# Moving the transposes of chunks 8 to 23 from TensorE to DMA, in a retention layer followed by a squared-ReLU feed-forward block

## The chip, the cores and the metric

The kernel runs on one core of a Trainium2 chip. The metric is the device time of one execution in microseconds (us). "Span" is the time from the first to the last instruction in the profile; a run takes about 1.8 us more than its span. Before: 227.94 us, median of 3 runs (227.5 to 228.03). PE is TensorE, PEld its weight loads, DVE is VectorE, ACT ScalarE, POOL GpSimd, and SPq is the instruction queue of SyncE, which issues most of the DMA transfers. "Half clock" below means that the profile shows a granted TensorE clock of 0.5.

## The reference

```python
# q, k, v: (4, 8, 768, 64), i.e. batch, heads, sequence, head dimension
gamma = 1.0 - 2.0 ** (-5.0 - np.arange(H))
for t in range(S):
    state = gamma * state + outer(k[t], v[t])          # per batch and head
    y[:, :, t] = (1/sqrt(64)) * q[t] @ state
x = y.transpose(0, 2, 1, 3).reshape(3072, 512)
h = np.maximum(x @ w_in, 0)                             # 512 -> 2048
out = (h * h) @ w_out                                   # 2048 -> 512
```

The kernel does the recurrence in 24 chunks of 128 time steps (6 per batch element). In a chunk, the scores of k against q are one matrix product, masked to the causal triangle; the state carries what came before. The decay is split into a factor on k and one on the query side. The feed-forward block is the bulk of the matmuls.

## The kernel before

For each chunk `m` a program string calls small steps: `K` casts, `T` transposes k and q, `S` makes the scores and masks them, `P` makes the output and the new state, `F` is a hidden tile (16 per block of chunks), `G` a quarter of an output tile, `Z` filler matmuls that keep TensorE busy at the start, `L` loads. The order is by hand: each engine executes its instructions in exactly this order.

```python
blocks = (2, 2, 1, 3, 4, 4, 4, 4)          # chunks per feed-forward block

def a_cast(m):                              # "K"
    nc.vector.scalar_tensor_tensor(out=ks[:], in0=kn.pop(m)[:], scalar=scale,
        in1=kf[:, i, :, None].to_broadcast([P, H, D]), op0=ALU.mult, op1=ALU.mult)
    if m < FIRST:                           # FIRST = 8
        # q: ScalarE for m < 4, GpSimd for 4 to 7; v: GpSimd
    ...                                     # from chunk 8 on the loads of q and v cast

def a_turn(m):                              # "T"
    for x, src in enumerate((a["ks"], a["qs"])):
        for p in range(NP):
            nc.tensor.transpose(tp[:, x, p, :], src[:, 2 * p : 2 * p + 2, :], ident[:])
    nc.scalar.activation(kqT[:], tp[:], AF.Copy)

def a_out(m, after=None):                   # "P"
    ...                                     # state, value and update matmuls
    nc.vector.tensor_tensor(out=xts[g][:, :, j * P : (j + 1) * P],
                            in0=yt[:], in1=yf[i][:], op=ALU.mult)   # yf: decay table
    ...
# yf[i] is filled by four Exp on ScalarE ("Y"), six tables in all
run("F0.0 P3 Y5 F0.1 F0.2 F0.3 F1.0 F1.1 F1.2 F1.3")
```

## Time and profile before

| | before |
|---|---|
| run, median | 227.94 us |
| span of the profile | 225.9 us |
| PE busy | 212.3 us, 94% |
| DVE, ACT busy | 46%, 54% |
| first hidden matmul | 19.46 us |
| first output matmul | 35.61 us |
| first hidden matmul of chunks 8 to 11 | 94.64 us |
| first hidden matmul of the last block | 194.48 us |
| end of the matmuls | 222.28 us |

The last rows are stage marks, read from the timeline of PE.

The page, part 1 (busy us, share of the span, instructions) and part 2 (busy tenths in 40 equal slices), kernel before:

```profile
PE 212.3 (94%) x1736; PEld 117.5 (52%) x1736; DVE 103.2 (46%) x221; ACT 123.1 (54%) x246; POOL 43.5 (19%) x62
...
PE   7677899998879999999999999999999999999993
```

From about the thirteenth slice on (some 68 us; a slice is 5.65 us) PE is full: there each microsecond of PE work taken away should come off the end. Before it, PE waits. The waits of PE, kernel before; the columns are the waiting instruction, what ended the wait, total us, times, longest:

```profile
PE tp_1119 L217 <- DVE ks_1116 L192: 1.3, 1, 1.3
PE hp_0_499 L316 <- ACT h_0_442 L323: 1.2, 1, 1.2
...
PE st_923 L227 <- ACT kqT_891 L218: 0.4, 1, 0.4
PE st_1055 L227 <- ACT kqT_1023 L218: 0.4, 1, 0.4
PE st_783 L227 <- ACT kqT_767 L218: 0.3, 1, 0.3
PE yt_862 L264 <- DVE pt_847 L235: 0.3, 1, 0.3
...
PE yt_981 L264 <- DVE pt_932 L235: 0.2, 1, 0.2
```

The 1.2 us of `hp_0_499` lies at 22.2 us, where ScalarE fills the last decay table:

The timeline of ACT, kernel before (start us, us, engine, line, operation):

```profile
20.87 0.77 ACT L297 ACTIVATE s_bd_174<-c_260 64x256 bf16<-64x256 f32 x2 [0.37 <-PE c_260 L280]
21.65 1.28 ACT L172 ACTIVATE yf_173<-t_f,lnp 128x128 f32<-128x128 f32 x4
22.95 0.38 ACT L323 ACTIVATE h_0_442<-hp_1_478 128x256 bf16<-128x256 f32 x1
```

The eviction of the second hidden tile starts only at 22.95 us, though that tile was made by 21.3 us; PE runs out of PSUM buffers (three for hidden and output tiles). What a chunk's transposes cost is seen where PE is full (timeline of PE, kernel before):

```profile
161.46 0.39 PE L217 MATMUL tp_2338<-ident,ks_2265 128*128 128x128 bf16 x4
161.69 0.39 PE L217 MATMUL tp_2338<-ident,qs_2079 128*128 128x128 bf16 x4
161.91 1.03 PE L316 MATMUL hp_0_2349<-xt_1995,w_in_bf_96 128*128 128x512 bf16 x4
```

From start to start the eight transposes hold PE for 161.91 - 161.46 = 0.45 us (0.445 over several chunks; the durations overlap, so they are not to be summed).

### The profile page before, as it was taken

The page shows a single profiled execution, that of the slowest core. Times are in us where ns is not written, and L with a number is a line of the kernel's source. Part 1 is how long each engine was busy: PE and PEld are TensorE (multiplying, and loading weights), DVE is VectorE, ACT ScalarE, POOL GpSimd, SP SyncE. Part 2 cuts the span into 40 slices and gives each one's busy share as a digit, 9 for nine tenths or more (in the row PEclk, how much of TensorE's full clock was granted, in tenths as well). Part 3 has the DMA queues.
Part 4 walks back from the last instruction along what each step waited for, and adds up shares of the span by engine and source line. Part 5 has one row for each costly group of instructions (what it writes and reads, how often), then busy time and mean ns, then how long its engine had stood idle before and what let it go on. Part 6 is the DMA issues. An engine that isn't in the chain of part 4 may idle for free.

```text
span 225.9 us, 4271 instructions
## 1 busy us (share of the span) xinstructions
PE 212.3 (94%) x1736; PEld 117.5 (52%) x1736; DVE 103.2 (46%) x221; ACT 123.1 (54%) x246; POOL 43.5 (19%) x62
## 2 busy tenths in 40 slices
PE   7677899998879999999999999999999999999993
PEld 2444785456646664445455555455454555444441
DVE  4574664127835964175650275740275704144000
ACT  6798883156637862377623477524467532367121
POOL 3275000439752433030330310000000000000000
PEclk9999999999999999999999999999999999999999
DMA  7999999989999999477729973013200011200112
GB/s 168 256 209 204 205 200 202 248 219 189 166 177 205 171 80 147 73 183 45 49 57 130 118 167 22 3 46 93 94 2 0 3 46 46 96 0 0 46 46 93
DMA packets 82579, 25.43 MB, mean 113 GB/s; under 512 B 75392, under 2 KB 79488, under 8 KB 82560
## 3 DMA queue, kind: packets, MB, share of 16 engines
q0 software_dynamic: 37504, 8.39, 40.7%
q1 hardware_dynamic: 45056, 16.78, 28.6%
q8 instruction: 13, 0.21, 0.4%
q14 instruction: 6, 0.05, 0.1%
HBM read 27.26 MB, written 6.29 MB: 149 GB/s over the span
## 4 chain that ended last, share of the span: by engine, by line
PE 84%; DMA 5%; ACT 4%; SPq 3%; DVE 2%; issue 1%; POOL 0%; ACTq 0%
DMA w_in_bf_96<-in_moe_w_in_dram 3%; SPq L91 3%; DMA vn_120<-in_v_dram 2%; PE op_2633 L335 2%; PE op_1480 L335 2%; PE op_2223 L335 2%; PE op_2512 L335 2%; PE op_2317 L335 2%; PE op_1920 L335 2%; PE op_1826 L335 2%; PE op_1427 L335 2%; PE op_1072 L335 2%; PE op_2860 L335 2%; PE op_705 L335 2%; PE op_695 L335 2%; PE op_2820 L335 2%
## 5 line engine op out<-in xcount | busy, mean ns | idle before, releaser
L316 PEld LDWEIGHTS <-w_in_bf_96 128*128 128x128 bf16 x128 | 11.4, 98 | 10.3 <-issue 1.4
L316 PEld LDWEIGHTS <-w_in_bf_98 128*128 128x128 bf16 x128 | 11.8, 98 | 8.7
L316 PEld LDWEIGHTS <-w_in_bf_99 128*128 128x128 bf16 x128 | 11.6, 98 | 8.2
L316 PEld LDWEIGHTS <-w_in_bf_97 128*128 128x128 bf16 x128 | 11.4, 98 | 8.1
L324 DVE TENSOR_TENSOR h_0_442<-h_0_442 128x256 bf16<-128x256 bf16 x32 | 9.3, 293 | 7.1 <-ACT h_0_442 L323 3.2
L324 DVE TENSOR_TENSOR h_5_2687<-h_5_2687 128x512 bf16<-128x512 bf16 x16 | 6.8, 426 | 11.8 <-ACT h_5_2687 L323 11.8
L324 DVE TENSOR_TENSOR h_2_1544<-h_2_1544 128x512 bf16<-128x512 bf16 x16 | 6.8, 424 | 10.7 <-ACT h_2_1544 L323 10.6
L324 DVE TENSOR_TENSOR h_4_2348<-h_4_2348 128x512 bf16<-128x512 bf16 x16 | 6.8, 425 | 9.6 <-ACT h_4_2348 L323 9.6
L324 DVE TENSOR_TENSOR h_3_1951<-h_3_1951 128x512 bf16<-128x512 bf16 x16 | 6.8, 423 | 9.5 <-ACT h_3_1951 L323 9.5
L324 DVE TENSOR_TENSOR h_1_876<-h_1_876 128x128 bf16<-128x128 bf16 (+1 forms) x32 | 8.2, 287 | 4.5 <-ACT h_1_876 L323 4.4
L335 PEld LDWEIGHTS <-h_5_2687 128*128 128x128 bf16 x64 | 6.3, 98 | 7.6
L335 PEld LDWEIGHTS <-h_3_1951 128*128 128x128 bf16 x64 | 6.0, 98 | 7.1
L335 PEld LDWEIGHTS <-h_2_1544 128*128 128x128 bf16 x64 | 6.0, 98 | 7.1
L335 PEld LDWEIGHTS <-h_4_2348 128*128 128x128 bf16 x64 | 5.9, 97 | 6.9
L335 PEld LDWEIGHTS <-h_1_876 128*128 128x128 bf16 x64 | 6.0, 98 | 6.8
L335 PEld LDWEIGHTS <-h_0_442 128*128 128x128 bf16 x64 | 6.0, 98 | 6.6
L351 PE MATMUL fill<-zero 128*128 128x512 bf16 x24 | 8.3, 484 | 1.2 <-DVE zero L146 1.2
L344 ACT ACTIVATE osb_744<-op_695 128x512 f32<-128x512 f32 x1 | 0.6, 597 | 8.2 <-PE op_695 L335 8.2
L253 PEld LDWEIGHTS <-s_bd_175 128*128 128x128 bf16 x48 | 3.6, 98 | 2.3
L351 PEld LDWEIGHTS <-zero 128*128 128x128 bf16 x24 | 2.4, 119 | 4.6 <-issue 2.7
L206 POOL CAST qs_736<-qn_420 128x512 bf16<-128x512 f32 x1 | 0.6, 613 | 19.6 <-DMA qn_420<-in_q_dram 19.6
L235 DVE TENSOR_TENSOR pt_792<-st_783,cmask 128x1024 bf16<-128x1024 f32 x1 | 1.2, 1225 | 5.8 <-PE st_783 L227 5.8
(811 smaller groups left out, 522.2 us busy)
## 6 DMA issues: line engine op xcount, KB each, us to landing
w_in_bf_96<-in_moe_w_in_dram POOLq DMA_DIRECT2D x1, 512.0 KB, 7.0
w_in_bf_97<-in_moe_w_in_dram POOLq DMA_DIRECT2D x1, 512.0 KB, 8.6
w_in_bf_98<-in_moe_w_in_dram POOLq DMA_DIRECT2D x1, 512.0 KB, 9.0
w_in_bf_99<-in_moe_w_in_dram POOLq DMA_DIRECT2D x1, 512.0 KB, 10.8
w_out_bf_100<-in_moe_w_out_dram POOLq DMA_DIRECT2D x1, 512.0 KB, 12.9
w_out_bf_101<-in_moe_w_out_dram POOLq DMA_DIRECT2D x1, 512.0 KB, 14.7
w_out_bf_102<-in_moe_w_out_dram POOLq DMA_DIRECT2D x1, 512.0 KB, 16.6
w_out_bf_103<-in_moe_w_out_dram POOLq DMA_DIRECT2D x1, 512.0 KB, 18.5
```

Of the source, the lines that this page charges most:

```text
L91: return eng.dma_start(t[:], src[b, :, i * C : (i + 1) * C, :].rearrange("h s d -> s h d"))
L206: nc.gpsimd.tensor_copy(qs[m][:], qn.pop(m)[:])
L235: nc.vector.tensor_tensor(out=pt[:], in0=st[:], in1=cmask[:, None, None, :].to_broadcast([P, 2, NP, P]), op=ALU.mult,)
L253: nc.tensor.matmul(yt[:, p, :], lhsT=s_bd[i % 2][:, p, :], rhs=kqT[:, 1, p, :], start=(p == 0), stop=False, skip_group_check=True,)
L316: nc.tensor.matmul(hp[:, :n], lhsT=w_in_bf[s][:, cb, r * P : (r + 1) * P], rhs=xts[g][:, cb, cols], start=(cb == 0), stop=(cb == NCB - 1),)
L324: nc.vector.tensor_mul(h2[:, fb, cols], h2[:, fb, cols], h2[:, fb, cols])
L335: nc.tensor.matmul(op[:], lhsT=h2s[g][:, fb, j * P : (j + 1) * P], rhs=w_out_bf[part][:, r, :], start=(fb == 0), stop=(fb == NFB - 1),)
L344: nc.scalar.activation(osb[:], op[:], AF.Copy)
L351: nc.tensor.matmul(t[:], lhsT=zero[:, :P], rhs=zero[:], start=True, stop=True)
```

## The change

Its intent: from chunk 8 on, k and q of a chunk, cast side by side into one tile, are transposed by one DMA transfer of 256 KB, issued by SyncE; TensorE and ScalarE are rid of it. The decay of the query side goes into the cast of q, on VectorE, so the decay tables and the multiplication of the output go; the output is copied by ScalarE. q is loaded as fp32 by SyncE (v still by the casting GpSimd queue), which gives SyncE four transfers a chunk: k, q, transpose, store. Blocks are 2-2-2-2-4-4-4-4. A 384-byte pad in front of the tiles aligns them. The PSUM buffer that was the transposes' own joins those of the hidden and output tiles, which become four. The schedule strings are rewritten. Cut to the core:

```diff
-    for n in (2, 2, 1, 3, 4, 4, 4, 4):
+    for n in (2, 2, 2, 2, 4, 4, 4, 4):
...
+    pad = wpool.tile([P, 192], BF16)
+    nc.vector.memset(pad[:], 0.0)
...
-    ps_f = ctx.enter_context(tc.tile_pool(name="ps_f", bufs=3, space=PS))
+    ps_f = ctx.enter_context(tc.tile_pool(name="ps_f", bufs=4, space=PS))
...
+    def q_cast(m):
+        nc.vector.tensor_tensor(
+            out=kq[m][:, 1], in0=raw.pop(("q", m))[:],
+            in1=qf[:, m % NCH, :, None].to_broadcast([P, H, D]), op=ALU.mult)
...
+    def dma_turn(m):
+        at[m] = kTpool.tile([P, 2, NP, P], BF16, tag="kqT", name=f"kqT{m}")
+        nc.sync.dma_start_transpose(
+            at[m][:].rearrange("d x p s -> d (x p) s"),
+            kq[m][:].rearrange("s x h d -> s (x h d)"))
...
-        nc.vector.tensor_tensor(out=xts[g][:, :, j * P : (j + 1) * P],
-            in0=yt[:], in1=yf[i][:], op=ALU.mult)
+        nc.scalar.activation(xts[g][:, :, j * P : (j + 1) * P], yt[:], AF.Copy)
...
+    run("k4 q4 v4 G0.3 t4 u4 G1.3 k5 q5 S4 G2.3 M4 t5 u5 v5 G3.0 P4 S5 M5 G3.1 L8 k6 q6 v6 G3.2 P5 G3.3 L9")
+    weave(all_f1(2), runs("t6 u6,k7 q7,S6 M6 v7,P6 t7 u7,S7 M7,k8 q8,P7 X8 L10"))
+    weave(all_f2(2), runs("k9 q9,X9 L11,k10 q10,S8 M8 L12,k11 q11"))
+    weave(all_f1(3), runs("X10,P8 S9 M9,X11 L13,P9 S10 M10 k12 q12"))
```

Letters now: `k`, `q`, `v` casts, `t`, `u` PE transposes of k and q, `X` the DMA transpose, `S` scores, `M` mask. `weave` spreads the comma-separated groups evenly between the feed-forward tiles.

## The prediction

> **What bounds it.** TensorE, in program order. The page shows PE busy 94% of a 225.9 us span; the chain of waits that ended last is 84% PE. The PE timeline has no gap after 66.3 us: four 128x512 matmuls take 0.864 us, over and over. Before that: up to 19.4 us PE waits for the first weights (issued at 12.47 us behind the cast of v2, 6.95 us to landing). From 19.4 to 35.6 us it runs the first hidden blocks, with one wait of 1.20 us for ScalarE, busy filling a decay table at 21.65 us. From 47 to 66 us, where chunks 4 to 7 pass attention beside narrow blocks, about 3.5 us go in waits on ACT and DVE, the longest 1.26 us for the cast of k6.
>
> **What changes, costed.**
> 1. PE transposes of chunks 8 to 23 go to DMA. Start to start, a chunk's eight hold PE for 0.445 us (161.46 to 161.91 us). 16 x 0.445 = 7.1 us, all in the gapless part, so all should come off the end. Their ACT evictions (1.02 us each) were off the path.
> 2. The decay tables go (24 Exp on ACT), and with them the 1.20 us wait. Casts of q by DVE (about 0.68 us) replace its output multiplies (0.69 us): level. ACT gets 24 evictions of about 0.6 us.
> 3. Start: same loads, same order, weights still behind the cast of v2: first hidden matmul stays near 19.4 us.
> 4. Blocks 2-2 instead of 1-3: four matmuls take 0.223, 0.437 and 0.651 us at 128, 256 and 384 columns; the sum is equal (14.0 us). In the new narrow block attention steps are two hidden tiles (0.87 us) apart, while a mask takes 1.22 us on DVE behind two casts: I keep 3 of the 3.5 us of waits.
> 5. DMA transposes, 16 x 256 KB on the SP queue among loads. No transpose in this trace gives a duration; plain loads of that size land in 2.9 to 5 us when quiet, up to 11.6 when crowded. The Trainium skill (Advanced Engine Details and Errata, X-Bar Transpose) expects 350 to 400 GB/s; no run here shows it yet. I estimate 4 to 5 us to landing. By program order PE leaves chunks 8 to 12 about 4.6 to 7.5 us between issue and first use, later chunks over 14 us. I allow 1 us of waits, at chunks 8 and 12.
> 6. q's casting DMAs become plain loads; the pad and pool order: nothing on the path.
>
> **Sum.** 225.9 - 7.1 - 1.2 - 0.5 + 1.0 = 218.1 us of span, plus the 1.75 us between span and run, less a little for a denser PE: 218.5 us (0.959), 80% range 215 to 223. Chances: faster by over 2% 0.88, within 2% 0.08, slower by over 2% 0.04.
>
> **Right or wrong shows as:** no PE transposes from chunk 8 on and PE gapless from about 70 us; PE's last block starting near 186.5 us (194.5 before); no ACT wait near 22 us; first hidden matmul near 19.4 us; waits of score matmuls on DMA transposes under 1.5 us in sum; transposes landing in 4 to 5 us.
>
> **What would make it wrong:** transposes of 8 us or more, or slowing the loads and stores that share their rings: chunks 8 to 12 would each stall PE by 2 to 3 us and cancel the gain. An SP queue held by a waiting transpose, delaying stores and so PSUM release. A PE pause before 19.4 us long enough to halve its clock (TensorE: Matmul & The Clock Gate, Part 1). The narrow block stalling more than before.

## The result, and the profile after

221.55 us, median of 4 runs (220.57 to 221.68), against 227.95 us of the kernel before: ratio 0.9714, 95% interval 0.9683 to 0.9744. A ratio here is the mean time of one kernel's fast runs over that of the other's of the same rounds, so it is not quite the ratio of the medians. The predicted 218.5 us was 3 us too low: of the 9.4 us that it forecast, 6.4 came, two thirds. The measured time lies in the predicted range.

| stage mark (us) | before | after | gain so far | gain in the stage |
|---|---|---|---|---|
| first hidden matmul | 19.46 | 19.67 | -0.21 | -0.21 |
| first output matmul | 35.61 | 34.45 | 1.16 | 1.37 |
| first hidden matmul of chunks 8 to 11 | 94.64 | 92.71 | 1.93 | 0.77 |
| first hidden matmul of the last block | 194.48 | 188.09 | 6.39 | 4.46 |
| end of the matmuls | 222.28 | 215.88 | 6.40 | 0.01 |

The page after the change, the same two parts:

```profile
PE 205.5 (93%) x1599; PEld 114.3 (52%) x1621; DVE 103.2 (47%) x213; ACT 112.4 (51%) x235; POOL 25.9 (12%) x41
...
PE   7987999999599979999999999999999999999992
```

(This trace holds 1599 of 1621 matmul records, so its PE busy time is read a little low; the stage marks do not suffer.) In the fourth row the stage holds the transposes of chunks 14 to 23, and 10 x 0.445 = 4.45 us: the gain is the removed PE work, to the digit. PE runs there with nothing where the transposes were (timeline of PE, after):

```profile
162.15 0.29 PE L277 MATMUL c_2108<-vs_1786,kq_1969 128*64 128x64 bf16 x8
162.38 0.40 PE L221 MATMUL st_2304<-kqT_2086 64*128 64x128 bf16 x8
162.71 1.04 PE L306 MATMUL hp_6_2315<-xt_1919,w_in_bf_102 128*128 128x512 bf16 x3
```

The third row is the odd one. It holds the transposes of chunks 8 to 13, 6 x 0.445 = 2.67 us, and gained only 0.77. The waits of PE after the change:

```profile
PE yt_947 L261 <- DVE pt_929 L233: 1.7, 1, 1.7
PE st_1318 L221 <- DMA kqT_1171<-kq_1117: 1.4, 1, 1.4
...
PE hp_0_409 L306 <- DMA w_in_bf_101<-in_moe_w_in_dram: 1.0, 1, 1.0
PE st_995 L221 <- ACT kqT_968 L206: 0.9, 1, 0.9
...
PE st_1131 L221 <- DMA kqT_1061<-kq_1020: 0.5, 1, 0.5
...
PE tp_1_739 L205 <- ACT osb_729 L334: 0.5, 1, 0.5
```

Between 43 and 82 us these are 1.72 (output of chunk 6), 1.45 (scores of chunk 10), 0.91 (scores of chunk 7), 0.54 (scores of chunk 8) and 0.46 (transposes of chunk 4): 5.08 us, where the kernel before had 2.90. The waits grew by 2.18 us. (The list also has gaps of 0.15 and 0.16 us, each beside a group of output matmuls that is one record short; e2_x10_early, whose trace has all 1621 records, does not show them, so they are not counted.) The hidden matmuls of the two equal blocks took 0.20 us less than those of the unequal ones, 14.51 against 14.71 us from start to start. So 2.67 + 0.20 - 2.18 = 0.69 of the 0.77 us are accounted for.

Two of them can be read further. The mask of chunk 6 (`pt_929`), timeline of DVE after the change:

```profile
54.58 0.68 DVE L176 SCALAR_TENSOR_TENSOR kq_903<-kn_675,kf 128x512 bf16<-128x512 f32 x1
55.18 0.68 DVE L186 TENSOR_TENSOR kq_903<-qn_677,qf 128x512 bf16<-128x512 f32 x1
55.79 0.48 DVE L314 TENSOR_TENSOR h_1_888<-h_1_888 128x256 bf16<-128x256 bf16 x2
56.19 1.22 DVE L233 TENSOR_TENSOR pt_929<-st_920,cmask 128x1024 bf16<-128x1024 f32 x1
```

Its scores were ready at 54.77 us (the matmuls start at 54.37 and take 0.40), but the casts of k7 and q7, and two squares of hidden tiles, stand ahead of it. And the DMA transpose of chunk 10 (`kqT_1171`), timeline of the SP queue:

```profile
67.29 2.47 SPq L210 DMA_TRANSPOSE kqT_1105<-kq_1097  x1
69.80 0.58 SPq L96 DMA_DIRECT2D kn_1107<-in_k_dram  x1
70.42 0.58 SPq L96 DMA_DIRECT2D qn_1109<-in_q_dram  x1
71.10 1.56 SPq L335 DMA_DIRECT2D out_dram<-osb_1128  x1
72.71 0.43 SPq L96 DMA_DIRECT2D kn_1142<-in_k_dram  x1
73.19 0.74 SPq L96 DMA_DIRECT2D qn_1144<-in_q_dram  x1
74.02 1.29 SPq L335 DMA_DIRECT2D out_dram<-osb_1168  x1
75.42 1.31 SPq L210 DMA_TRANSPOSE kqT_1171<-kq_1117  x1
```

Its cast was done at 71.57 us; it was issued at 75.42, behind two stores and a load pair. The queue hands out one transfer after the other, and a transpose takes it 1.2 to 3.6 us. The DMA view gives the time from issue to landing of the transposes:

```profile
kqT_1171<-kq_1117 SPq DMA_TRANSPOSE x1, 5.7
...
kqT_1521<-kq_1497 SPq DMA_TRANSPOSE x1, 6.7
...
kqT_2256<-kq_2231 SPq DMA_TRANSPOSE x1, 2.7
```

It is 2.7 us when the loads are over. Among loads and stores, chunks 8 to 11 take 5.0 to 6.0 us, the later ones 2.8 to 6.7.

### The profile page after: what moved, and what is told of

Read it like the earlier page. It is cut to its first block, busy times and chain, and to the rows that moved or that the text cites. A ratio compares the mean times of both kernels' runs of the same rounds, so it can differ in the third digit from the quotient of the medians.

```text
span 219.9 us, 3991 instructions
## 1 busy us (share of the span) xinstructions
PE 205.5 (93%) x1599; PEld 114.3 (52%) x1621; DVE 103.2 (47%) x213; ACT 112.4 (51%) x235; POOL 25.9 (12%) x41
## 4 chain that ended last, share of the span: by engine, by line
PE 80%; DMA 10%; SPq 3%; ACT 2%; DVE 1%; issue 1%; POOL 0%; ACTq 0%
SPq L96 3%; DMA w_in_bf_101<-in_moe_w_in_dram 3%; DMA kqT_1171<-kq_1117 3%; DMA kqT_1061<-kq_1020 2%; DMA vn_125<-in_v_dram 2%; PE op_2495 L325 2%; PE op_1148 L325 2%; PE op_691 L325 2%; PE op_788 L325 2%; PE op_1375 L325 2%; PE op_2475 L325 2%; PE op_1766 L325 2%; PE op_2131 L325 2%; PE op_2722 L325 2%; PE op_2420 L325 2%; PE op_2154 L325 2%
## 5 line engine op out<-in xcount | busy, mean ns | idle before, releaser
L306 PEld LDWEIGHTS <-w_in_bf_101 128*128 128x128 bf16 x128 | 12.2, 98 | 10.1 <-DMA w_in_bf_101<-in_moe_w_in_dram 1.5
L306 PEld LDWEIGHTS <-w_in_bf_103 128*128 128x128 bf16 x128 | 12.4, 98 | 8.4
L306 PEld LDWEIGHTS <-w_in_bf_104 128*128 128x128 bf16 x128 | 12.2, 98 | 7.9
L306 PEld LDWEIGHTS <-w_in_bf_102 128*128 128x128 bf16 x128 | 12.2, 98 | 7.9
L314 DVE TENSOR_TENSOR h_5_2549<-h_5_2549 128x512 bf16<-128x512 bf16 x16 | 6.8, 426 | 18.0 <-ACT h_5_2549 L313 18.0
L341 PE MATMUL fill<-zero 128*128 128x512 bf16 x35 | 11.7, 461 | 1.4 <-DVE zero L146 1.3
L314 DVE TENSOR_TENSOR h_0_408<-h_0_408 128x256 bf16<-128x256 bf16 x32 | 9.3, 293 | 7.7 <-ACT h_0_408 L313 4.0
L314 DVE TENSOR_TENSOR h_1_888<-h_1_888 128x256 bf16<-128x256 bf16 x32 | 8.0, 288 | 6.8 <-ACT h_1_888 L313 6.2
L314 DVE TENSOR_TENSOR h_4_2234<-h_4_2234 128x512 bf16<-128x512 bf16 x16 | 6.8, 426 | 9.0 <-ACT h_4_2234 L313 9.0
L314 DVE TENSOR_TENSOR h_3_1881<-h_3_1881 128x512 bf16<-128x512 bf16 x16 | 6.7, 425 | 7.5 <-ACT h_3_1881 L313 7.5
L325 PEld LDWEIGHTS <-h_5_2549 128*128 128x128 bf16 x64 | 6.2, 97 | 7.6
L325 PEld LDWEIGHTS <-h_4_2234 128*128 128x128 bf16 x64 | 6.1, 98 | 7.3
L325 PEld LDWEIGHTS <-h_3_1881 128*128 128x128 bf16 x64 | 6.1, 98 | 7.3
L325 PEld LDWEIGHTS <-h_2_1506 128*128 128x128 bf16 x64 | 6.1, 98 | 7.3
L325 PEld LDWEIGHTS <-h_1_888 128*128 128x128 bf16 x64 | 6.0, 98 | 6.7
L325 PEld LDWEIGHTS <-h_0_408 128*128 128x128 bf16 x64 | 5.9, 98 | 6.5
L314 DVE TENSOR_TENSOR h_2_1506<-h_2_1506 128x512 bf16<-128x512 bf16 x16 | 6.3, 422 | 2.7 <-ACT h_2_1506 L313 2.7
L341 PEld LDWEIGHTS <-zero 128*128 128x128 bf16 x37 | 3.7, 114 | 5.2 <-issue 3.0
L250 PEld LDWEIGHTS <-s_bd_163 128*128 128x128 bf16 x48 | 3.7, 98 | 2.2
L233 DVE TENSOR_TENSOR pt_2209<-st_2200,cmask 128x1024 bf16<-128x1024 f32 x1 | 1.2, 1225 | 5.6 <-PE st_2200 L221 5.6
L233 DVE TENSOR_TENSOR pt_1850<-st_1841,cmask 128x1024 bf16<-128x1024 f32 x1 | 1.2, 1224 | 5.6 <-PE st_1841 L221 5.6
```

Of the source, the lines that this page charges most:

```text
L233: nc.vector.tensor_tensor(out=pt[:], in0=st[:], in1=cmask[:, None, None, :].to_broadcast([P, 2, NP, P]), op=ALU.mult,)
L250: nc.tensor.matmul(yt[:, p, :], lhsT=s_bd[i % 2][:, p, :], rhs=kqT[:, 1, p, :], start=(p == 0), stop=False, skip_group_check=True,)
L306: nc.tensor.matmul(hp[:, :n], lhsT=w_in_bf[s][:, cb, r * P : (r + 1) * P], rhs=xts[g][:, cb, cols], start=(cb == 0), stop=(cb == NCB - 1),)
L314: nc.vector.tensor_mul(h2[:, fb, cols], h2[:, fb, cols], h2[:, fb, cols])
L325: nc.tensor.matmul(op[:], lhsT=h2s[g][:, fb, j * P : (j + 1) * P], rhs=w_out_bf[part][:, r, :], start=(fb == 0), stop=(fb == NFB - 1),)
L341: nc.tensor.matmul(t[:], lhsT=zero[:, :P], rhs=zero[:], start=True, stop=True)
```

## The experiments

Twelve kernels ran. Each kernel has one profile, and in these the first hidden matmul comes anywhere between 19.5 and 21.3 us, so a kernel's own effect is read from its stages in the profile; "stage" is from the first hidden matmul to the end of the matmuls, 202.82 us before and 196.21 us after. Run times are given beside it. The record calls a run "slow" when it is over 1.5% above the fastest of its kernel, and takes ratios from the other runs alone, so a kernel whose own waits lower its clock is flattered; where that happened it is said. All results were correct.

### e1_pe_turn: the transposes back on PE, all else kept

```diff
             elif op == "X":
-                dma_turn(*args)
+                a_turn(*args, 0)
+                a_turn(*args, 1)
```

> The changed kernel with each DMA transpose of chunks 8 to 23 replaced, at the same place of the program, by the eight PE transposes and two ScalarE evictions that chunks 0 to 7 have. Theory (the transposes were pure PE work, the DMA form costs only its two waits): 16 x 0.445 = 7.1 us of PE comes back and the waits of the score matmuls on DMA transposes (0.54 and 1.45 us in the profile) go, so 5 us slower than the changed kernel, about 226.5 us, ratio to the kernel before about 0.994. Rival (the DMA transposes also cost something hidden, by crowding loads and stores): clearly less than 4 us slower, 225 us or below.

230.38 us (230.16 to 232.78), ratio 1.0138 (1.0053 to 1.0222): the interval lies above 1, but not clear of 2%, so the record's verdict is "unclear". The expected 226.5 us was missed. The stage is 204.49 us, 8.28 more than after the change; I had expected 5. The waits of PE on DMA transposes went, as expected (1.99 us), and 16 x 0.445 = 7.12 us of PE work came back; the other 3.15 us are waits and small gaps that I had not counted. All of them lie before 97 us, 1.57 us of them in the list of waits, on casts. From there to the last block, where PE is full, the stage takes 99.40 us instead of 95.38: 4.02 us, the nine transposes and nothing else. In the timeline of PE:

```profile
67.91 0.40 PE L205 MATMUL tp<-ident,kq 128*128 128x128 bf16 x4 [0.58 <-DVE kq L176]
68.51 0.40 PE L205 MATMUL tp<-ident,kq 128*128 128x128 bf16 x4 [0.20 <-DVE kq L186]
```

An `X` stands right behind the casts that it needs. As a PE instruction it holds TensorE until the casts are done; as a DMA transfer it waits in SyncE's queue instead, and TensorE goes on. So in this program order, which was written for the DMA form, that form is worth the PE work plus, in the stretch that is not full, that decoupling. The rival, a hidden cost of the DMA transposes, has nothing in its favour: the stage of ten chunks gained all of its 4.45 us.

### e2_x10_early: one DMA transpose ahead in its queue

```diff
-    weave(all_f2(2), runs("k9 q9,X9 L11,k10 q10,S8 M8 L12,k11 q11"))
-    weave(all_f1(3), runs("X10,P8 S9 M9,X11 L13,P9 S10 M10 k12 q12"))
+    weave(all_f2(2), runs("k9 q9,X9 L11,k10 q10 X10,S8 M8 L12,k11 q11"))
+    weave(all_f1(3), runs(",P8 S9 M9,X11 L13,P9 S10 M10 k12 q12"))
```

> The changed kernel with the DMA transpose of chunk 10 put right behind its q cast, ahead of one load pair and one store on the SP queue. Theory (it was late because it stood in the in-order SP queue: issued at 75.42 us, 3.9 us after its cast was done): issued near 71.6 us, landed before 78 us, the 1.45 us wait of the score matmul of chunk 10 gone, about 220.1 us. Rival (the landing time of a transpose in crowded rings is what costs): the wait moves to a later transpose or a cast, and the time stays within 0.3 us of 221.5.

The q cast of chunk 10 started at 72.31 us and took 0.69, so it ended at 73.00; the transpose was issued 0.07 us later, where the change had issued it 3.85 us after its cast. The timeline of the SP queue in this run:

```profile
71.86 0.58 SPq L96 DMA_DIRECT2D qn<-in_q_dram  x1
73.07 2.09 SPq L210 DMA_TRANSPOSE kqT<-kq  x1
75.25 0.52 SPq L335 DMA_DIRECT2D out_dram<-osb  x1
```

The wait of the scores of chunk 10 is gone (the only one on a DMA transpose left is the 0.6 us of chunk 8). The stage is 194.73 us, 1.48 shorter, which is the 1.45 us wait and no more: nothing took its place. The run time alone would not have shown it: 221.1 us (220.41 to 222.79), ratio 0.9707, since the runs scatter: in the profiled one the first hidden matmul came at 21.04 us. The wait was a matter of the queue's order.

### e3_mask_first: the mask ahead of two casts

```diff
-    weave(all_f1(2), runs("t6 u6,k7 q7,S6 M6 v7,P6 t7 u7,S7 M7,k8 q8,P7 X8 L10"))
+    weave(all_f1(2), runs("t6 u6,,S6 M6 v7 k7 q7,P6 t7 u7,S7 M7,k8 q8,P7 X8 L10"))
```

> The changed kernel with the casts of k7 and q7 moved behind the mask of chunk 6 in VectorE's order. Theory (the 1.72 us wait at the output of chunk 6 comes from two casts, 1.2 us, standing ahead of the mask in the in-order engine): that wait falls to 0.3 to 0.5 us, some 0.3 to 0.6 us come back as a wait of the transposes of chunk 7 for the casts; net about 0.7 us faster, 220.8 us. Rival (ScalarE feeds VectorE late, the casts have room anyway): the wait stays above 1.2 us and the time does not move.

```profile
56.97 0.41 PE L261 MATMUL yt<-pt,vs 128*64 128x128 bf16 x8 [0.66 <-DVE pt L233]
58.17 0.40 PE L205 MATMUL tp<-ident,kq 128*128 128x128 bf16 x4 [0.20 <-DVE kq L186]
```

In this timeline of PE the wait fell from 1.72 to 0.66 us, and 0.20 us came back at the next transposes. The wait of the scores of chunk 7 also fell, from 0.91 to 0.40 us, and that of chunk 10 rose from 1.45 to 1.63. The stage is 195.28 us, 0.93 shorter; 220.53 us (219.3 to 222.08), ratio 0.9674. The casts ahead of the mask made most of that wait. The other 0.66 us are not the rival's: VectorE works without a pause up to the mask, which starts 0.37 us after its scores, behind squares, and takes 1.22 us itself, while PE has only two hidden tiles (0.87 us) to do.

### e4_y5_late: the kernel before, with one decay table filled later

```diff
-    run("F0.0 P3 Y5 F0.1 F0.2 F0.3 F1.0 F1.1 F1.2 F1.3")
+    run("F0.0 P3 F0.1 F0.2 F0.3 F1.0 F1.1 F1.2 F1.3")
     ...
     run(" ".join(f"G{m}.{s}" for s in (0, 1, 2) for m in (0, 1, 2)))
+    run("Y5")
```

> The kernel before with only the last decay table (four Exp, 1.28 us of ScalarE) moved from behind the output of chunk 3 to behind the last output block before chunk 4, where ScalarE idles for 8 us. Theory: the 1.20 us PE wait at 22.2 us goes and nothing else moves, 226.75 us, ratio 0.995. Rival (PE is then held by the weights or by the square of the hidden tiles instead): less than 0.5 us.

From the first hidden to the first output matmul 14.87 us instead of 16.15, and the whole stage 1.28 us shorter: the 1.20 us wait came from that table alone. The change got 14.78 us there. The run times do not show it: 226.64 and 226.65 us twice, but 229.49 and 229.68 twice, ratio 1.0004 (0.9914 to 1.0093). The profile of this kernel has 3.41 us of half clock at 14.3 us, before the first hidden matmul; but it is of a run of 226.65 us, so that does not explain the two long runs, which have no profile. More of the clock below.

### e5_blocks13: the old block sizes in the new schedule

```diff
-    for n in (2, 2, 2, 2, 4, 4, 4, 4):
+    for n in (2, 2, 1, 3, 4, 4, 4, 4):
```

> The changed kernel with the old block sizes 2-2-1-3 and its own schedule strings. Judged by stages (start of the first hidden matmul to the end of TensorE), since the start of runs scatters. Theory (the hidden work is equal, but the narrower block leaves the attention chain of chunks 6 and 7 and the first DMA transposes half the cover): the waits grow by 2 to 3 us and the stage is 2 to 3 us longer than the changed kernel's 196.2 us. Rival (as the prediction costed it: equal work, no effect): within 0.5 us.

226.84 us (225.99 to 227.85), ratio 0.9925; the stage is 201.85 us, 5.6 longer. More than expected, and for another reason. The clock line of its page:

```profile
PEclk9998899999679999999999999999999999999999
```

The trace's clock record has half clock for 3.41 us near 20 us and for 6.83 us near 60 us; the profile after the change has none before its end. Of the 5.6 us, 1.55 lie in the first stage (16.33 us instead of 14.78), where PE had waited 2.00 us for the first weights and then ran at half clock: this belongs to the start, not to the blocks. Of the rest, 4.1 us, lying between 54 and 99 us, the waits on the timeline of PE are 5.23 us against 4.62 in that stretch after the change, only 0.6 us more. The other 3.5 us go with the 6.83 us of half clock, which can cost up to half its length, 3.4 us (about 3.0, an estimate, since PE stood idle for 0.8 us of it). So the narrow block does not add much waiting; the larger cost is a drop of the clock. That it drops at this place in every run is not shown; all four runs have a mean clock of 0.977 to 0.985.

When it drops can be read from the fourteen traces together. After the clock's first rise its record changes only at multiples of 3.41 us from that rise, and what counts is how long PE is idle inside one such stretch. In all six stretches at full clock with 1.75 us of idle PE or more (here 1.75 and 2.00, elsewhere up to 3.41), half clock followed; in none with 1.67 us or less; between 1.71 and 1.74 us it followed once in seven times. A wait that lies across a boundary counts in two parts. In e2_x10_early the wait of 1.98 us for the first weights did, and the clock stayed (windows view; the number after the comma is PE's busy time):

```profile
16.61:20.02 3.41, 2.05 (x32) 1.12 (x31) 1.57 (x2) 1.54 (x4) 3.41 (x6) 1.00 1.22 196
20.02:23.44 3.42, 2.40 (x35) 2.10 (x36) 0.58 (x2) 1.51 (x4) 1.28 (x2) 1.00 1.24 205
```

Here, 1.54 us of the 1.94 us wait for the mask of chunk 6 and two small waits fell into one stretch, and made the 1.75 us. The kernel after the change has 1.53 us in that place. So it was a close thing, and whether the block sizes or the place of the boundary decided it is not shown.

### e6_q_pool: the q casts of chunks 4 to 7 on GpSimd

```diff
     def q_cast(m):
-        nc.vector.tensor_tensor(
+        eng = nc.gpsimd if 4 <= m < FIRST else nc.vector
+        eng.tensor_tensor(
```

> The changed kernel with the q casts of chunks 4 to 7 on GpSimd, where the kernel before had them, instead of VectorE. Theory (moving these casts to VectorE is what lengthened the wait before the output of chunk 6 from 0.20 to 1.72 us): that wait falls by about 0.7 us, the length of one cast; stage 0.5 to 1 us shorter if the GpSimd form takes under 1.5 us. Rival (GpSimd multiplies so slowly, over 2 us, that the transposes wait for it instead): as long or longer.

GpSimd takes 1.04 us for it (VectorE 0.69). The wait at the output of chunk 6 fell from 1.72 to 1.11 us, by one cast, as expected; the stage is 195.46 us, 0.75 shorter; 220.84 us (220.62 to 221.72), ratio 0.9682 (0.9654 to 0.9709). The kernel before had these casts on GpSimd (0.61 us each), and no wait of PE in its list ended on them.

### e7_xt_dve: the output copy on VectorE

```diff
-        nc.scalar.activation(xts[g][:, :, j * P : (j + 1) * P], yt[:], AF.Copy)
+        nc.vector.tensor_copy(xts[g][:, :, j * P : (j + 1) * P], yt[:])
```

> The changed kernel with the copy of the attention output (one per chunk) on VectorE instead of ScalarE. Theory (on ScalarE it stands in front of the eviction of the next transposes, and makes most of the 0.91 us wait of the score matmul of chunk 7): that wait falls by 0.4 to 0.6 us, nothing else moves, stage 0.4 to 0.6 us shorter. Rival (VectorE is the tighter engine there): another wait on VectorE grows by as much, no gain.

The wait of the scores of chunk 7 fell from 0.91 to 0.61 us, the other waits stayed (1.72, 1.37, 0.58); the stage is 195.88 us, 0.33 shorter. The direction is right, the size is below what was expected: the copy makes a third of that wait, not most of it. In run time it is lost: 222.22 us, ratio 0.9728 (0.9701 to 0.9755).

### e8_tuned: the order mended for chunks 4 to 11, first try

```diff
-    run("k4 q4 v4 G0.3 t4 u4 G1.3 k5 q5 S4 G2.3 M4 t5 u5 v5 G3.0 P4 S5 M5 G3.1 L8 k6 q6 v6 G3.2 P5 G3.3 L9")
-    weave(all_f1(2), runs("t6 u6,k7 q7,S6 M6 v7,P6 t7 u7,S7 M7,k8 q8,P7 X8 L10"))
-    weave(all_f2(2), runs("k9 q9,X9 L11,k10 q10,S8 M8 L12,k11 q11"))
-    weave(all_f1(3), runs("X10,P8 S9 M9,X11 L13,P9 S10 M10 k12 q12"))
+    run("k4 q4 v4 G0.3 t4 G1.3 u4 k5 q5 G2.3 S4 M4 t5 G3.0 u5 v5 k6 q6 P4 S5 M5 G3.1 L8 v6 k7 q7 G3.2 P5 t6 u6 G3.3 L9")
+    weave(all_f1(2), runs(",S6 M6 v7,t7 u7,P6,S7 M7,k8 q8 X8 L10,P7,"))
+    weave(all_f2(2), runs("k9 q9 X9 L11,S8 M8,k10 q10 X10 L12,k11 q11"))
+    weave(all_f1(3), runs("X11 L13,P8 S9 M9,,P9 S10 M10 k12 q12"))
```

> The changed kernel with its program order mended in one stretch only (chunks 4 to 11): transposes spread between output tiles, casts of k6, q6, k7, q7 before the masks they used to delay, transposes of chunk 6 before the narrow block, DMA transposes put right behind their casts. No work added or removed. Theory (the 5 us of waits that the changed kernel has between 43 and 82 us are order, not work): 3 to 4.5 us of them go, about 217.5 us, ratio to the kernel before about 0.955, faster than both. Rival (DMA bandwidth in that stretch sets when casts can run): under 1.5 us.

A miss. The hidden stage of the narrow block became 9.85 us instead of 12.51, its waits gone. But I had drawn the scores of chunk 8 forward by two groups, and its DMA transpose, issued at 60.93 us, had not landed:

```profile
61.98 1.03 PE L325 MATMUL op<-w_out_bf,h 128*128 128x512 bf16 x4
67.70 0.61 PE L221 MATMUL st<-kqT 64*128 64x128 bf16 x8 [4.69 <-DMA kqT<-kq]
```

PE waited 4.69 us; the score matmuls behind it took 0.61 us instead of 0.40, half clock for 6.83 us. The profiled run counts as slow (222.4 us of span, clock 0.98), but by the kernel's own wait; the three fast ones gave ratio 0.9683 (0.9631 to 0.9735), the six runs, 219.29 to 224.16 us, have a mean of 0.974: no gain over the change.

### e9_fill_more: more filler before the first hidden matmul

```diff
-    run("k3 t3 q3 Z3 u3 Z2 M2 S3 P2 v3 Z3 M3")
+    run("k3 t3 q3 Z3 u3 Z2 M2 S3 P2 v3 Z9 M3")
```

> The changed kernel with six more filler matmuls (1.3 us) in the gap before the first hidden matmul, where TensorE waits 1.0 to 2.0 us for the first weights. Theory (the scatter of the runs comes from that gap: where it nears 2 us the granted clock drops and the next stage, first hidden to first output matmul, takes 16.3 instead of 14.78 us, as in the profile of e5_blocks13): every run keeps clock 0.995 or more, the first hidden matmul is not later, the runs spread under 1 us, median 221 us or a little below. Rival (the scatter comes from when the loads land): the spread stays, and the start is delayed where weights come early; no gain.

No gain: 222.33 us (221.69 to 224.04), ratio 0.9762 (0.9728 to 0.9796), and two of six runs have a mean clock of 0.991 and 0.992, the mark of one stretch of half clock. The first hidden matmul came at 19.80 us in the profile. The theory that the gap at the start makes the scatter is not borne out. The rival is, for the start: in 12 of the 14 traces the first hidden matmul starts 0.04 to 0.05 us after the first weights have landed, and they land anywhere from 19.42 to 21.28 us. Here they had landed at 19.19, and the filler held PE until 19.80. What makes the rest of the scatter stays open.

### e10_tuned2: the order mended, second try

```diff
-    weave(all_f2(2), runs("k9 q9 X9 L11,S8 M8,k10 q10 X10 L12,k11 q11"))
-    weave(all_f1(3), runs("X11 L13,P8 S9 M9,,P9 S10 M10 k12 q12"))
+    weave(all_f2(2), runs("k9 q9 X9 L11,,k10 q10 X10 L12,"))
+    weave(all_f1(3), runs("S8 M8,k11 q11 X11 L13,P8 S9 M9,,P9 S10 M10 k12 q12"))
```

(against e8_tuned, and with `Z9` as in e9_fill_more)

> e8_tuned with the score matmul of chunk 8 moved back from two output tiles before to the start of the next hidden block, since its DMA transpose could not land before 67.7 us there and held TensorE for 4.69 us, and with the six more fillers. Theory (order, not work): the waits between 43 and 82 us fall from the changed kernel's 5 us to under 1.5 us; first hidden matmul to the first of the group of chunks 8 to 11 falls from 73.0 to about 69.5 us; 218 us, ratio to the kernel before about 0.956, faster than both. Rival (DMA bandwidth sets when the casts of chunks 9 to 11 can run, so another wait takes the place of this one): 220 us or more.

220.06 us, median of 7 runs (218.88 to 224.33); the fast runs have ratio 0.9639 (0.9606 to 0.9672). That beats the kernel before and, by intervals that do not overlap, the change (0.9683 to 0.9744), but by less than half of what I expected. Two of the seven runs count as slow, the profiled one among them; over all seven the ratio of the means is 0.968, so that the order beats the change in every run is not shown. In the profile the waits of chunks 4 to 10 are nearly gone (the longest is 0.27 us), and a new one is there, the scores of chunk 11 on their DMA transpose:

```profile
85.14 0.61 PE L221 MATMUL st<-kqT 64*128 64x128 bf16 x8 [2.94 <-DMA kqT<-kq]
```

That transpose was issued at 77.45 us, behind two stores and 1.3 us after its cast, and landed 7.6 us later, the longest of all. So the rival has a share in it: with the chunks drawn closer, the time to landing in this stretch becomes the limit, and one wait takes the place of another. In the profiled slow run it is thus the kernel's own wait that ends in half clock (the other slow run has no profile), so a reader who adopts the order should also give chunk 11 more room; that was not tried.

### e11_nopad: without the pad

```diff
-    pad = wpool.tile([P, 192], BF16)
-    nc.vector.memset(pad[:], 0.0)
```

> The changed kernel without the 384-byte pad in front of the weights, so without its aligned tiles. Theory (nothing on the path depends on it): the same stage times within 0.3 us, median within 0.5 us of the changed kernel's. Rival (alignment speeds the DMA of weights or loads): the first weights, or the transposes, land over 0.5 us later and the waits on them grow.

The rival was right on the packets; on the time it stays open. 223.79 us (222.64 to 224.84), ratio 0.9812 (0.9775 to 0.9849), outside the interval of the change. From 2 to 12 us, where the twelve first loads run, the windows view says (busy time of each engine, clock, DMA share, GB/s), first for the kernel after the change, then for e11_nopad:

```profile
2.00:12.00 10.00, 9.43 (x75) 4.75 (x75) 5.41 (x8) 3.57 (x10) 1.27 (x3) 1.00 1.09 247
```

```profile
2.00:12.00 10.00, 8.61 (x72) 4.18 (x71) 4.74 (x7) 3.56 (x10) 1.27 (x3) 1.00 1.29 222
```

The DMA engines are busier (a share above 1 means that packets of one engine overlap) and move less. In the trace's DMA records the 256-byte packets that start in this window take 23.6 ns on average, against 17.9 after the change and 18.0 before (a shorter stretch, the first 7 us of these loads, gives 22.9 against 17.9). In the built program's addresses the loaded tiles start at 0 modulo 512 bytes after the change, at 256 before, and at 128 without the pad. The first weights are issued at 14.16 us instead of 12.91, later than in any of the other traces (12.47 to 13.30). They land at 20.55 us, and the first hidden matmul comes at 20.60 instead of 19.67 us; that lies within the scatter of the others. The transposes are slower too: the quickest of this trace lands in 3.03 us, those of the other ten traces with DMA transposes in 2.70 to 2.74. Further on, the wait for the transpose of chunk 10 is 2.1 us instead of 1.45, and there a stretch of half clock follows: that stage takes 13.09 us instead of 10.75.

### e12_pad128: a pad of 128 bytes

```diff
-    pad = wpool.tile([P, 192], BF16)
+    pad = wpool.tile([P, 64], BF16)
```

> The changed kernel with a pad of 128 bytes instead of 384. In the built program's addresses all loaded and transposed tiles then start at 256 modulo 512, where the changed kernel has 0 and e11_nopad 128. Theory (what e11_nopad lost, 2.2 us, is 256-byte packets that no longer start on a 256-byte boundary; 256 is enough, as the load tiles of the kernel before show, which lie at 256 and have 18.0 ns packets): packets of the first loads take 18 ns as in the changed kernel, not 23.1 as in e11_nopad, GB/s from 2 to 12 us about 245, not 222, time 221 to 222 us. Rival (512 is needed, or the loss of e11_nopad was chance): 223 us or more; or packets at 18 ns but the time still at 223.8.

Packets of the first loads: 17.9 ns (the 23.1 of the expectation was taken over a shorter stretch), and 242 GB/s from 2 to 12 us. So a start on a 256-byte boundary is enough for the packets, as the theory had it. The time is inconclusive: 222.81 us (221.44 to 224.22), ratio 0.9749 (0.9697 to 0.9801), an interval that takes in both the change and e11_nopad. The profiled run has half clock at the start (a wait of 2.3 us for the first weights, then 16.13 us to the first output matmul instead of 14.78); one more run has the same mean clock, 0.99, and no profile. How much of the 2.2 us of e11_nopad is alignment and how much is chance of the clock stays open; that its packets are slower is shown.

## Why the prediction was right or wrong

**The bound: right.** PE in program order. Where PE was full before, the gain of a stage is the PE work taken out of it: 4.46 us for ten chunks.

**Transposes, 7.1 us: right as PE work.** 0.445 us a chunk; e1_pe_turn shows that at the new places of the program the DMA form is worth even 8.28 us net, since a PE transpose right behind its casts also waits for them. They did lie in the gapless part of the kernel before; but "so all should come off the end" failed for the first six, since after the change that stretch (the third row) has waits of its own.

**The decay table, 1.2 us: right.** 1.37 us in that stage after the change, 1.28 us in e4_y5_late, which moves that table and nothing else.

**The start, "first hidden matmul stays near 19.4 us": right in the profile** (19.67), but it scatters up to 21.3 us from profile to profile, which I did not see coming.

**"I keep 3 of the 3.5 us of waits": right in sum, by luck, and from a wrong base.** By the timeline's list there were 2.90 us, so the 0.5 us that the prediction takes off was not there to take. After the change the waits without those on DMA transposes are 3.09 us, but they are other waits: the longest of before, 1.26 us for the cast of k6, is gone, and 1.72 us for the mask of chunk 6 is new. The prediction had named a mask behind two casts (1.22 us against 0.87 us of hidden tiles) and put no cost on it. It had reckoned VectorE as "level", over the whole kernel: casts of q in, output multiplies out. But for chunks 4 to 7 the q casts came from GpSimd, and on VectorE they landed ahead of a mask that PE waits for; and the output copy landed on ScalarE ahead of the evictions of the next transposes. e3_mask_first (-0.93 us), e6_q_pool (-0.75) and e7_xt_dve (-0.33) each take a part of it back; they overlap, so they are not to be summed.

**DMA transposes, "4 to 5 us to landing", "1 us of waits, at chunks 8 and 12": the term that was mis-sized most.** Landing took 2.7 us when quiet, just under the plain loads, and 5 to 6.7 us for most in the crowd. The waits were 1.99 us, twice the 1 us, at chunks 8 and 10. I had counted the room from issue to first use, 4.6 to 7.5 us for chunks 8 to 12, by the order of the program of PE. From the end of its cast to the moment when PE wanted it, chunk 10 had 8.1 us (71.57 to 79.70), but its queue issued it 3.85 us late, and it landed 5.7 us after that. The Trainium skill (Advanced Engine Details and Errata, X-Bar Transpose) expects 350 to 400 GB/s. 256 KB at that rate would be 0.7 us, an estimate from the page's figure; the quiet transposes here take 2.7 us from issue to landing. The DMA records of one of them (kqT_2086, the 256-byte packets) run from 1.18 to 2.26 us after its issue: 256 KB in 1.08 us are 243 GB/s, below the page's figure, and 1.6 of the 2.7 us lie before the first packet and after the last.

**"The pad: nothing on the path": wrong as a statement on the pad.** Without it the packets take 23.6 ns; what that costs in time is not shown. It is no gain over the kernel before, whose load tiles were aligned by luck of the sizes in front of them; it keeps the change from losing this.

**"The sum is equal" for blocks 2-2 and 1-3: right for the work, wrong for the effect.** e5_blocks13 is 4.1 us longer in that stretch, about 0.6 us of it in waits and most of the rest beside half clock, of which it is open whether the blocks bring it.

**The sum.** The terms gave 218.1 us of span and 1.75 us on top, 219.85. I then wrote 218.5, "less a little for a denser PE": 1.35 us for which no number stood. That is nearly half of the error of 3.05 us. The measured span is 219.9 us, 1.8 above the terms. Of the waits, which grew by 2.18 us where I had allowed 0.5, come 1.68: 0.99 from those on DMA transposes, 0.6 from the base of 3.5, 0.09 from the rest. The start (0.21 us later) and the stretch after the last matmul (4.0 us instead of 3.6) add 0.6, the table and the hidden tiles give back 0.4; the sum is right to about 0.1 us.

**Its own marks.** It had said by what it would show. No PE transposes from chunk 8 on, no ACT wait near 22 us, the first hidden matmul near 19.4 us: so it came. PE without gaps from about 70 us, the last block near 186.5 us, waits on DMA transposes under 1.5 us, landing in 4 to 5 us: not so (a wait up to 81.15 us, 188.09 us, 1.99 us, 2.7 to 6.7 us).

## What to carry to other kernels

When work moves between engines, do not balance it over the whole kernel: look, stage by stage, at which instruction stands right behind the new place, and whether the engine that waits for that instruction is the bottleneck. A DMA that takes work off an engine buys that work and also decouples it from its inputs, but its latency counts from when its queue gets to it: put it directly behind its input in the queue's order, ahead of stores and loads that nobody waits for. Read a change whose size is near the scatter of the runs by stage marks in the profile, and check after each move of the memory layout that loaded tiles still start on a 256-byte boundary: off it, the packets here took a third longer. Where PE has to wait, keep the wait short: from 1.75 us within one 3.41 us stretch on, half clock followed each time here.

## What the Trainium skill lacked or had wrong

- DMA: Bandwidth & Descriptors, How a descriptor splits into AXI transactions: it says that a transaction must start from a 256-byte-aligned address, and tells the cost of a start off that boundary in beats. No figure is given for a load whose SBUF side alone is off it. Here, with 256-byte packets, 23.6 ns instead of 17.9 at a tile start of 128 modulo 256 (e11_nopad), and 17.9 again at 256 modulo 512 (e12_pad128). The page's rules for kernel authors do not mention tile alignment.
- Advanced Engine Details and Errata, X-Bar Transpose: it gives a bandwidth and no latency. Here a 256 KB transpose from SBUF to SBUF holds the SP queue for 1.2 to 3.6 us and lands 2.7 us after issue when quiet, 2.8 to 6.7 us among loads and stores (7.6 in e10_tuned2). The packets of a quiet one make 243 GB/s, not 350 to 400.
- TensorE: Matmul & The Clock Gate, Part 1, gives a window of 3413 ns. The trace agrees: its stretches of half clock are 3.41 or 6.83 us long. The page's section on why this matters advises against PE idle gaps over about 3 us; here a wait of 2.0 us (e5_blocks13) and one of 2.3 us (e12_pad128) were followed by half clock, while 2.0 us in e2_x10_early and 1.6 us in e10_tuned2 were not. So a gap of 2 us is already a risk: what counted in these traces was 1.75 us or more of idle PE inside one 3.41 us stretch of the clock's record (see e5_blocks13).
- No page has the cost of a PE transpose that stands right behind its casts: e1_pe_turn lost 8.28 us for 7.12 us of transposes and 1.99 us of waits saved, so 3.15 us by waiting for inputs and small gaps, all before the stretch where PE is full.
